# Attention followed by a max-of-three feed-forward: the last 64 queries summed in 64x64 tiles, and output tiles stored by one transfer

## Chip, cores and metric

The kernel runs on one core of one Trainium2 chip. The metric is the device time in microseconds (us). The kernel before took 341.37 us (median of 8 runs, 341.04 to 341.73).

## What is computed

`q`, `k` and `v` have 8 batches, 12 heads, 448 positions and head size 64, in float32. The attention is a softmax whose denominator has one more term; its result is laid out as 3584 tokens of 768 features and goes through a feed-forward part with three weight matrices and a maximum.

```python
scores = scale * np.matmul(q, k.transpose(0, 1, 3, 2))      # scale = 1/8
m = np.max(scores, axis=-1, keepdims=True)
e = np.exp(scores - m)
attn = e / (np.sum(e, axis=-1, keepdims=True) + np.exp(-m) + 1e-09)
x = np.matmul(attn, v)                                       # to (3584, 768)
h = np.maximum(np.maximum(x @ w1, x @ w2), x @ w3)
out = h @ w_out
```

## The kernel before

All matmuls are in float16 with float32 sums. The kernel leaves the maximum out: it computes exp(scores) and divides by the sum plus 1, which is the same quotient but for the 1e-09. Values carry a 65th column of 1/256, so that one matmul gives the weighted sum and the denominator, both scaled alike (L161, L162).

**Groups.** The 12 heads of a batch go in 3 groups of 4 heads, so there are 24 groups `i`. The 448 positions are taken as 7 rows of 64. The 4 heads are two pairs `pr`, and the 4 windows `w` of a head's queries hold 128, 128, 128 and 64 queries: the last window is half empty. Keys are taken in blocks of two rows of 64 (X1, X2, X3 in L274) and one tail row `TL`, for which both heads of a pair share one block.

**One group.** Loads come from GpSimd's queue (`load_qk`, `load_v`), three to four groups ahead, and cast to float16. From group 7 on two DMA transposes on SyncE's queue (SP) turn queries and keys (`transpose_dma`, L233, issued two groups ahead), and GpSimd shifts parts of the queries between partition halves (`shift_q`, four copies, L245). Scores (L300) are 64x64 tiles of TensorE, their exponential is ScalarE's (L320) and is written to one of two buffers `e`.

**Attention times values.** `av` (L528) works on one pair of heads and one accumulator tile `avp`, which is two PSUM banks from a pool of three tiles shared with the scores. `av_tail` (L330) adds the tail row for the four windows as 16 tiles of 64x64. `av_main` (L349) adds the three full blocks as 2 heads x 4 windows x 3 blocks = 24 matmuls of 128x128 by 65 columns. VectorE then computes the denominators (L367), their reciprocals (L370) and the product for all four windows and both heads (L373), into `xn`.

**Feed-forward.** `xn` of a group goes to `xT`, from group 6 on by one DMA transpose on SP (`x_transpose_dma`, L421). The work of the feed-forward is cut in pieces: `up_piece` is six matmuls into one of two PSUM tiles of the pool `ps_b` and a copy or a running maximum by VectorE (L449, L451); `out_piece` is six matmuls for half of a 128-row output tile (L464), scaled by VectorE into one of six buffers `o_sb` (L471). After the second half the tile is stored.

**Order.** The order is written by hand. Each group `i` from 3 on has three visits `vi` with 2, 2 and 3 score units (loop at L620). The first two visits also run `av` of the group before. After that `fill` (L511) issues pieces from a list until a credit in matmul columns is used up; `share` (L606) spreads what is left evenly over the visits up to the next batch. The engines work through their own instructions in this order. At the end (L670) come the two last `av`, the last transpose of `xn`, the rest of the pieces and those of the last batch.

**Stores.** A 128-row output tile holds two rows of 64 tokens, whose places in the output are 7 tokens apart, and the two halves start at different tokens. Each half is stored by its own transfer of 64 partitions, both from SP (L481); the last tile goes in three cuts, partly from ScalarE's queue.

Of the kernel before, what the change touches and what calls it, by code (L numbers as in the profile page):

```python
# [10 lines left out]
FP32 = mybir.dt.float32  # L11
FP16 = mybir.dt.float16
AF = mybir.ActivationFunctionType
ALU = mybir.AluOpType
ts = bass.ts

MMDT = FP16
# [4 lines left out]
def kernel(  # L22
# [33 lines left out]
    PE_QK = 7  # L56
    NF = 3
    PE_X = 2
    NEB = 2
    NV = 3  # L60

    cpool = ctx.enter_context(tc.tile_pool(name="const", bufs=1))
    att_pool = ctx.enter_context(tc.tile_pool(name="att", bufs=3))
    small = ctx.enter_context(tc.tile_pool(name="small", bufs=3))
    xn_pool = ctx.enter_context(tc.tile_pool(name="xn", bufs=3))
    xt_pool = ctx.enter_context(tc.tile_pool(name="xt", bufs=3))
    ht_pool = ctx.enter_context(tc.tile_pool(name="ht", bufs=2))
    out_pool = ctx.enter_context(tc.tile_pool(name="outp", bufs=6))
# [94 lines left out]
    for j in range(NEB):  # L163
        nc.vector.memset(e_buf[j][:, NB * S : NB * S + HP], 0.0)
        blk = e_buf[j][:, 0 : NB * S].rearrange("p (n s) -> p n s", s=2 * S)
        nc.vector.memset(blk[:, :, NO : NO + HP], 0.0)

    def warm(n, cols=512):
        ps = ps_b.tile([128, 512], FP32, tag="b", name="warm")
# [152 lines left out]
    def e_col(n, w):  # L322

        return n * S + ((192, 320, 0, 128) if n % 2 == 0 else (0, 128, 256, 384))[w]
# [5 lines left out]
    def av_tail(i, ej, pr, ws=(0, 1, 2, 3)):  # L330

        eF, vt = e_buf[ej], vt_buf[i % NV]
        ps = ps_s.tile([128, 2, 512], FP32, tag="s", name="avp")
        avs[i, pr] = ps
        n = where[pr, None, TL]
        for j, w in enumerate(ws):
            for hh in range(2):
                for half in range(2):
                    o = e_col(n, w) + half * HP
                    nc.tensor.matmul(  # L340
                        out=ps[half * HP : half * HP + HP, hh, j * D1 : (j + 1) * D1],
                        lhsT=eF[hh * HP : hh * HP + HP, o : o + HP],
                        rhs=vt[hh * HP : hh * HP + HP, pr, 0:D1],
                        start=(j == 0),
                        stop=False,
                        skip_group_check=True,
                    )

    def av_main(i, ej, pr, ws=(0, 1, 2, 3)):  # L349
        eF, vx = e_buf[ej], v_buf[i % NV]  # L350
        ps = avs.pop((i, pr))
        nw = len(ws)
        for hh in range(2):
            for j, w in enumerate(ws):
                for c, x in enumerate((X1, X3, X2)):
                    o = e_col(where[pr, hh, x], w)
                    nc.tensor.matmul(  # L357
                        out=ps[:, hh, j * D1 : (j + 1) * D1],
                        lhsT=eF[:, o : o + 128],
                        rhs=vx[:, 2 * pr + hh, (x[0]), 0:D1],  # L360
                        start=False,
                        stop=(c == 2),
                        skip_group_check=True,
                    )
        acc = ps[:, :, 0 : nw * D1].rearrange("p h (j d) -> p h j d", d=D1)
        rb = small.tile([P, 2, 4], FP32, tag="rb", name="rb")
        nc.vector.tensor_scalar(  # L367
            out=rb[:, :, 0:nw], in0=acc[:, :, :, D], scalar1=1.0 / LAMBDA, scalar2=None, op0=ALU.add
        )
        nc.vector.reciprocal(out=rb[:, :, 0:nw], in_=rb[:, :, 0:nw])  # L370
        if i not in xn:
            xn[i] = xn_pool.tile([P, NP, 4, 2, D], MMDT, tag="xn", name="xn")
        nc.vector.tensor_tensor(  # L373
            out=xn[i][:, pr, ws[0] : ws[0] + nw].rearrange("p j h d -> p h j d"),
            in0=acc[:, :, :, 0:D],
            in1=rb[:, :, 0:nw].unsqueeze(3).to_broadcast([P, 2, nw, D]),
            op=ALU.mult,
        )

    def prep_v(i, eng):  # L380
        t = raw[i]["v"]
        vx, vt = v_buf[i % NV], vt_buf[i % NV]
        eng.tensor_copy(out=vx[:, :, :, 0:D], in_=t[:, :, 1:4, :])  # L383
        t2 = t.rearrange("p (r h) t d -> p r h t d", r=NP)
        eng.tensor_copy(out=vt[0:HP, :, 0:D], in_=t2[0:HP, :, 0, 4, :])
        eng.tensor_copy(out=vt[HP:P, :, 0:D], in_=t2[HP:P, :, 1, 0, :])
# [34 lines left out]
    def x_transpose_dma(i):  # L421
        b, g = groups[i]
        nc.sync.dma_start_transpose(
            out=xt_tile(b)[:, 2 * g : 2 * g + 2, :].rearrange("p a (j s) -> p (a j) s", s=128),
            in_=xn[i].rearrange("p a j h d -> p (a j h d)"),
        )
# [26 lines left out]
    NW = DM // 2  # L453
    order = (0, 2, 4, 6, 1, 3, 5)

    def out_piece(bp, t, c, w, queues):

        if c == 0:
            outs[0] = out_pool.tile([128, DM], FP32, tag="o_sb", name="o_sb")
            outs[1] = 0  # L460
        o_sb = outs[0]
        op_ps = ps_b.tile([128, 512], FP32, tag="b", name="op_ps")
        for fc in range(NFC):
            nc.tensor.matmul(  # L464
                out=op_ps[:, 0:w],
                lhsT=hT[bp][:, fc, ts(t, 128)],
                rhs=wout_sb[:, fc, c : c + w],
                start=(fc == 0),
                stop=(fc == NFC - 1),
            )  # L470
        nc.vector.tensor_scalar(  # L471
            out=o_sb[:, c : c + w], in0=op_ps[:, 0:w], scalar1=1.0 / LAMBDA, scalar2=None,
            op0=ALU.mult,
        )
        if queues is None:
            return
        for half in range(2):
            n = 2 * t + half
            b = 2 * bp + n // T
            rows = out[b * S : (b + 1) * S].rearrange("(p t) m -> t p m", t=T)[order[n % T]]  # L480
            queues[half].dma_start(  # L481
                out=rows[:, outs[1] : c + w], in_=o_sb[half * HP : half * HP + HP, outs[1] : c + w]
            )
        outs[1] = c + w


# [9 lines left out]
    def add_out(b):  # L496
        sy, sc = nc.sync, nc.scalar
        for t in range(0, 3) if b % 2 == 0 else range(3, 7):
            cuts = [(0, NW, None), (NW, NW, (sy, sy))]
            if b == B - 1 and t == 6:  # L500
                cuts = [(0, NW, (sy, sy)), (NW, 256, (sc, sc)), (NW + 256, 128, (sy, sc))]
            for c, w, queues in cuts:
                pieces.append((out_piece, (b // 2, t, c, w, queues), NFC * (w + 6)))

    def add_batch(b):
        add_up(b, 0, S, [(i, fc) for fc in range(NFC) for i in range(3)])
# [4 lines left out]
    def fill(cols):  # L511
# [5 lines left out]
        if not pieces:  # L517
            credit[0] = min(credit[0], 0.0)

    def left():  # L520
        return sum(w for _, _, w in pieces)

# [3 lines left out]
    STEP = 2 * NDC * (NO + 6)  # L526

    def av(i, ej, pr, part):  # L528
        av_tail(i, ej, pr, PW[part])
        av_main(i, ej, pr, PW[part])  # L530

# [88 lines left out]
    for i in range(3, NI):  # L620
        ej, pj = (i + 1) % NEB, i % NEB
        first = i == 3
        if PE_QK <= i + 2 < NI:
            transpose_dma(i + 2)
        if first:
            load_v(i + 2)
        for vi, units in enumerate(visits):
            n = 3 * i + vi
            scores(i, ej, units)
            if i == 4 and vi == 0:  # L630
                prep_v(i, DV)
            if vi < 2:
                av(i - 1, pj, vi, "E" if first else "EO")
            if vi == 1 and i > 3 * PE_X:
                x_transpose_dma(i - 1)
            if n in adds:
                add_batch(adds[n])
            per = STEP if first and vi < 2 else share(n)
            if vi == 0 and first:
                x_transpose_pe(1, "E")  # L640
            if vi == 2 and first:
                x_transpose_pe(i - 1, "E")
                fill(per / 2)
                prep_v(i, DV)
                for w, cols in ((0, (0, NE)), (1, (0, NE)), (2, (NE, NO)), (2, (0, NE))):
                    add_up(0, *cols, [(w, f) for f in (0, 2, 4)])
                add_out(0)
                per = share(n)
            if vi == 2 and 3 < i <= 3 * PE_X:
                x_transpose_all(i - 1)  # L650
            if first:
                fill(per)
                per = 0
            if i + 1 < PE_QK and vi < 2:
                transpose_once(i + 1, "qk"[vi], (AC, DV)[vi])
            fill(per)
        if i + 1 < PE_QK:
            shift_q(i + 1, nc.gpsimd)
        if first:
            load_qk(i + 3)  # L660
        if i < 5:
            load_more(i + 3, i + 4)
        if 5 <= i + 1 < NI:
            prep_v(i + 1, nc.gpsimd)
        if PE_QK <= i + 2 < NI:
            shift_q(i + 2, nc.gpsimd)
        if i >= 5:
            load_more(i + 3, i + 4)

    av(NI - 1, NI % NEB, 0, "EO")  # L670
    av(NI - 1, NI % NEB, 1, "EO")
    x_transpose_dma(NI - 1)
    fill(float("inf"))
    add_batch(B - 1)
# [31 lines left out]
```

The softmax here doesn't subtract the row's maximum and nothing guards it: scores larger than these inputs give would overflow.

## Time and profile before

| | us |
|---|---|
| median of 8 runs (range) | 341.37 (341.04 to 341.73) |
| profiled execution, its own time | 341.04 |
| its span, first to last instruction | 339.2 |
| TensorE busy, matmuls | 329.2 |
| VectorE busy | 188.5 |
| ScalarE busy | 151.1 |
| GpSimd busy | 146.4 |

The profile is one execution with times from the hardware. "L357" is a line of the kernel; `avp<-vx,e` names what is written and read. PE is TensorE's matmuls, PEld its weight loads, DVE VectorE, ACT ScalarE, POOL GpSimd, SPq the queue of SyncE. A group's line gives the count, the busy time, the mean of one in ns, and the idle time before it with what ended it. Matmuls overlap in a pipeline, so the pace of a row of them is read from the starts, and not from the mean of one. The mean granted clock of TensorE was 0.999 of full speed. DMA lines give a queue's packets, megabytes, and the time that its packets took as a share of the 16 DMA engines; issue lines give the count, the size of one and the median time from issue to landing.

### The profile page before, as it was taken

The numbers are of one execution on the slowest core, as the hardware profiler recorded it, in microseconds if no ns is written. First come the engines' busy times: TensorE is split into PE (matmuls) and PEld (weight loads), VectorE is DVE, ScalarE is ACT, GpSimd is POOL, SyncE is SP. The second block draws the span as 40 slices with busy tenths as digits, with TensorE's granted clock in tenths as the row PEclk, the third lists the DMA queues.
The fourth block names the chain that finished last, engine by engine and source line by source line (L and its number), as shares of the span: only waits on it lengthen the run. The fifth ranks groups of instructions, "written<-read, shape, count | busy, mean of one in ns | idle before, by whom it ended". The sixth has DMA issues, their size and how long they took to land.

```text
span 339.2 us, 9812 instructions
## 1 busy us (share of the span) xinstructions
PE 329.2 (97%) x4172; PEld 198.9 (59%) x4172; DVE 188.5 (56%) x410; ACT 151.1 (45%) x181; POOL 146.4 (43%) x260
## 2 busy tenths in 40 slices
PE   7899999999999999999999999999999999999994
PEld 3678788765555655555555645555555655555552
DVE  4556665565546555555545555546456556465552
ACT  4868856653554545453543445463543454200000
POOL 8595669882735177065265271936162000000000
PEclk9999999999999999999999999999999999999999
DMA  8999999999997997989988999999960440133006
GB/s 148 194 186 206 201 206 179 151 165 206 126 128 107 216 213 103 127 135 208 138 102 108 209 199 106 156 138 197 150 119 20 116 116 3 31 79 95 0 19 167
DMA packets 84812, 46.42 MB, mean 137 GB/s; under 512 B 53280, under 2 KB 81312, under 8 KB 84768
## 3 DMA queue, kind: packets, MB, share of 16 engines
q0 software_dynamic: 29120, 21.80, 48.2%
q1 hardware_dynamic: 55264, 23.60, 38.1%
q8 instruction: 32, 0.52, 0.6%
q10 hardware_dynamic: 384, 0.39, 0.4%
q14 instruction: 12, 0.10, 0.1%
HBM read 44.04 MB, written 11.01 MB: 162 GB/s over the span
## 4 chain that ended last, share of the span: by engine, by line
PE 91%; ACT 2%; DVE 2%; DMA 2%; issue 1%; POOL 1%; POOLq 0%; ACTq 0%
PE p_i L440 48%; PE op_ps L464 16%; PE avp L357 11%; PE stp L300 11%; PE avp L340 2%; ACT e L320 2%; DMA ld_q<-in_q_dram 2%; DVE xn L373 1%; PE trT L225 1%; DVE QT L186 1%; PE xtp L413 0%; ACT QT L184 0%; DVE rb L370 0%; POOL ld_k L102 0%; PE xtp L400 0%
## 5 line engine op out<-in xcount | busy, mean ns | idle before, releaser
L320 ACT ACTIVATE e<-stp 128x896 f16<-128x896 f32 (+4 forms) x171 | 144.2, 904 | 137.0 <-PE stp L300 136.8
L440 PE MATMUL p_i<-xT,w 128*128 128x448 f16 (+2 forms) x972 | 173.4, 332 | 0.2
L440 PEld LDWEIGHTS <-w 128*128 128x128 f16 x972 | 90.0, 98 | 68.2 <-issue 5.4
L245 POOL COPY QT<-QT 64x384 f16<-64x384 f16 (+1 forms) x84 | 46.7, 556 | 93.5 <-DMA QT<-ld_q 71.6
L451 DVE TENSOR_TENSOR hT<-hT,p_i 128x448 f16<-128x448 f16 (+2 forms) x96 | 59.6, 621 | 43.1 <-PE p_i L440 42.9
L464 PE MATMUL op_ps<-w,hT 128*128 128x384 f16 (+2 forms) x342 | 58.1, 323 | 0.0
L300 PE MATMUL stp<-QT,KT 64*64 64x448 f16 (+2 forms) x756 | 48.1, 338 | 2.6 <-ACT e L320 0.9
L464 PEld LDWEIGHTS <-hT 128*128 128x128 f16 x342 | 32.1, 98 | 23.0 <-issue 2.0
L357 PE MATMUL avp<-vx,e 128*128 128x65 f16 x1152 | 45.4, 193 | 0.0
L471 DVE TENSOR_SCALAR o_sb<-op_ps 128x384 f32<-128x384 f32 (+2 forms) x57 | 31.3, 550 | 23.7 <-PE op_ps L464 23.1
L449 DVE CAST hT<-p_i 128x448 f16<-128x448 f32 (+2 forms) x48 | 30.0, 625 | 24.4 <-PE p_i L440 24.4
L357 PEld LDWEIGHTS <-e 128*128 128x128 f16 x1152 | 38.8, 97 | 2.3
L373 DVE TENSOR_TENSOR xn<-avp,rb 128x512 f16<-128x512 f32 (+1 forms) x54 | 34.1, 632 | 1.9
L300 PEld LDWEIGHTS <-KT 64*64 64x64 f16 x756 | 15.9, 105 | 27.1 <-issue 24.3
L367 DVE TENSOR_SCALAR rb<-avp 128x8 f32<-128x8 f32 (+1 forms) x54 | 8.9, 165 | 40.2 <-PE avp L357 40.1
L383 POOL COPY vx<-ld_v 128x768 f16<-128x768 f16 x21 | 17.2, 818 | 7.6 <-issue 4.4
L340 PEld LDWEIGHTS <-e 64*64 64x64 f16 x768 | 14.8, 107 | 7.9 <-issue 1.4
L102 POOL DMA_DIRECT2D ld_q<-in_q_dram x24 | 17.5, 730 | 2.5 <-DMA w<-in_moe_w_out_dram 1.7
L102 POOL DMA_DIRECT2D ld_k<-in_k_dram x24 | 17.4, 727 | 2.1 <-PE p_i L440 1.3
L115 POOL DMA_DIRECT2D ld_v<-in_v_dram x24 | 15.2, 634 | 3.2 <-DMA w<-in_moe_w_dram 1.9
L340 PE MATMUL avp<-vt,e 64*64 64x65 f16 x768 | 15.4, 192 | 0.6 <-ACT e L320 0.4
L112 POOL DMA_DIRECT2D ld_v<-in_v_dram x24 | 15.2, 635 | 1.6 <-DMA w<-in_moe_w_dram 1.6
(43 smaller groups left out, 86.0 us busy)
## 6 DMA issues: line engine op xcount, KB each, us to landing
out_dram<-o_sb SPq DMA_DIRECT2D x54, 192.0 KB, 3.5
ld_v<-in_v_dram POOLq DMA_DIRECT2D x48, 128.0 KB, 4.3
ld_k<-in_k_dram POOLq DMA_DIRECT2D x23, 224.0 KB, 6.6
ld_q<-in_q_dram POOLq DMA_DIRECT2D x23, 224.0 KB, 7.0
w<-in_moe_w_dram POOLq DMA_DIRECT2D x9, 384.0 KB, 9.4
w<-in_moe_w_out_dram POOLq DMA_DIRECT2D x3, 384.0 KB, 8.7
xT<-xn SPq DMA_TRANSPOSE x18, 3.9
QT<-ld_q SPq DMA_TRANSPOSE x17, 5.0
```

Source lines behind the costliest of these rows:

```text
L102: nc.gpsimd.dma_start(out=tiles[nm][:, 1 : NP * T + 1].rearrange("x (r t) d -> x r (t d)", r=NP)[:, p0:p1], in_=src[:, p0:p1],)
L245: eng.tensor_copy(out=t[d0 : d0 + HP, o * 128 : (o + n) * 128], in_=t[s0 : s0 + HP, a * 128 : (a + n) * 128],)
L300: nc.tensor.matmul(out=stp[half * HP : half * HP + HP, par, j * qn : (j + 1) * qn], lhsT=k_block(i, pr, h2, x[half]), rhs=q_cols(i, pr, h2 ...
L320: nc.scalar.activation(out=dst, in_=src, func=AF.Exp, scale=scale)
L340: nc.tensor.matmul(out=ps[half * HP : half * HP + HP, hh, j * D1 : (j + 1) * D1], lhsT=eF[hh * HP : hh * HP + HP, o : o + HP], rhs=vt[hh * ...
L357: nc.tensor.matmul(out=ps[:, hh, j * D1 : (j + 1) * D1], lhsT=eF[:, o : o + 128], rhs=vx[:, 2 * pr + hh, (x[0]), 0:D1], start=False, stop= ...
L373: nc.vector.tensor_tensor(out=xn[i][:, pr, ws[0] : ws[0] + nw].rearrange("p j h d -> p h j d"), in0=acc[:, :, :, 0:D], in1=rb[:, :, 0:nw]. ...
L440: nc.tensor.matmul(out=p_i[:, j * qn : (j + 1) * qn], lhsT=w_sb[i][:, dc, ts(fc, 128)], rhs=xT[b][:, dc, q0 : q0 + qn], start=(dc == 0), s ...
L449: nc.vector.tensor_copy(out=dst, in_=src)
L451: nc.vector.tensor_tensor(out=dst, in0=dst, in1=src, op=ALU.max)
L464: nc.tensor.matmul(out=op_ps[:, 0:w], lhsT=hT[bp][:, fc, ts(t, 128)], rhs=wout_sb[:, fc, c : c + w], start=(fc == 0), stop=(fc == NFC - 1),)
L471: nc.vector.tensor_scalar(out=o_sb[:, c : c + w], in0=op_ps[:, 0:w], scalar1=1.0 / LAMBDA, scalar2=None, op0=ALU.mult,)
```

## The change

There are two parts.

*Sums of the last window.* From group 6 on (`LAST`), `av_tail` and `av_main` cover windows 0 to 2 alone. A new function `av_last` computes window 3 as 64x64 tiles: the contraction's two halves go to two row halves of TensorE and to two banks, and the two heads to two partition halves. So each bank holds half of the sum. ScalarE copies the second bank's half out of PSUM (`end`); one piece of the feed-forward is issued (`one`); then `finish` lets VectorE add the first bank's half, compute the denominator and reciprocal, and ScalarE scale the two heads into `xn`. The transpose of `xn` is issued after `finish`. The unused partitions of `xn` are set to zero once, so `xn` becomes three fixed buffers.

*Stores.* An output tile is stored by one transfer with a target of two runs of 64 rows, where the second half's token follows the first's (`r1 > r0`); otherwise by two transfers as before. Of seven tiles per two batches one (t = 5) stays with two.

```diff
@@ setup
+    LAST = 6
...
-    xn_pool = ctx.enter_context(tc.tile_pool(name="xn", bufs=3))
...
+    xn_buf = [cpool.tile([P, NP, 4, 2, D], MMDT, name=f"xn{j}") for j in range(NV)]
+    for j in range(NV):
+        nc.vector.memset(xn_buf[j][HP:P, :, 3], 0.0)
@@ new
+    def av_last(i, ej, pr):
+        eF, vx, vt = e_buf[ej], v_buf[i % NV], vt_buf[i % NV]
+        ps = avs[i, pr]
+
+        def tile_mm(r, hh, o, rhs, stop):
+            nc.tensor.matmul(
+                out=ps[hh * HP : hh * HP + HP, r, 3 * D1 : 4 * D1],
+                lhsT=eF[r * HP : r * HP + HP, o : o + HP],
+                rhs=rhs,
+                start=False,
+                stop=stop,
+                skip_group_check=True,
+            )
+
+        n = where[pr, None, TL]
+        for hh in range(2):
+            tile_mm(hh, hh, e_col(n, 3), vt[hh * HP : hh * HP + HP, pr, 0:D1], False)
+        for c, x in enumerate((X1, X3, X2)):
+            for r in range(2):
+                for hh in range(2):
+                    o = e_col(where[pr, hh, x], 3)
+                    rhs = vx[r * HP : r * HP + HP, 2 * pr + hh, x[0], 0:D1]
+                    tile_mm(r, hh, o, rhs, c == 2)
@@ av_main, after the product for the windows given
+        if not last:
+            return None
+        end = small.tile([P, D1], FP32, tag="end", name="end")
+        rl = small.tile([P, 1], FP32, tag="rl", name="rl")
+        nc.scalar.activation(out=end, in_=ps[:, 1, 3 * D1 : 4 * D1], func=AF.Copy)
+
+        def finish():
+            nc.vector.tensor_tensor(out=end, in0=ps[:, 0, 3 * D1 : 4 * D1], in1=end, op=ALU.add)
+            nc.vector.tensor_scalar(
+                out=rl, in0=end[:, D:], scalar1=1.0 / LAMBDA, scalar2=None, op0=ALU.add
+            )
+            nc.vector.reciprocal(out=rl, in_=rl)
+            for hh in range(2):
+                h = slice(hh * HP, hh * HP + HP)
+                nc.scalar.activation(
+                    out=xn[i][0:HP, pr, 3, hh], in_=end[h, 0:D], func=AF.Copy, scale=rl[h]
+                )
+
+        return finish
@@ out_piece
-        for half in range(2):
-            n = 2 * t + half
-            b = 2 * bp + n // T
-            rows = out[b * S : (b + 1) * S].rearrange("(p t) m -> t p m", t=T)[order[n % T]]
-            queues[half].dma_start(
-                out=rows[:, outs[1] : c + w], in_=o_sb[half * HP : half * HP + HP, outs[1] : c + w]
-            )
+        r0, r1 = ((2 * bp + n // T) * S + order[n % T] for n in (2 * t, 2 * t + 1))
+        cols = slice(outs[1], c + w)
+        for p0, r, k in ((0, r0, 2),) if r1 > r0 else ((0, r0, 1), (HP, r1, 1)):
+            at = out[r : r + 1, cols]
+            rows = bass.AP(
+                at.tensor, at.offset, [[abs(r1 - r0) * DM, k], [T * DM, HP], [1, c + w - outs[1]]]
+            )
+            queue.dma_start(out=rows, in_=o_sb[p0 : p0 + k * HP, cols])
@@ add_out: the last tile's cuts
-                cuts = [(0, NW, (sy, sy)), (NW, 256, (sc, sc)), (NW + 256, 128, (sy, sc))]
+                cuts = [(0, NW, sy), (NW, 256, sc), (NW + 256, 128, sy)]
@@ planner
+    def one():
+        if pieces:
+            fill(max(0.0, 1.0 - credit[0]))
...
     def av(i, ej, pr, part):
+        if i >= LAST:
+            av_tail(i, ej, pr, (0, 1, 2))
+            av_last(i, ej, pr)
+            return av_main(i, ej, pr, (0, 1, 2), True)
@@ loop over visits
+            finish = None
             if vi < 2:
-                av(i - 1, pj, vi, "E" if first else "EO")
-            if vi == 1 and i > 3 * PE_X:
-                x_transpose_dma(i - 1)
+                finish = av(i - 1, pj, vi, "E" if first else "EO")
             if n in adds:
                 add_batch(adds[n])
             per = STEP if first and vi < 2 else share(n)
+            if finish:
+                one()
+                finish()
+            if vi == 1 and i > 3 * PE_X:
+                x_transpose_dma(i - 1)
@@ end
-    av(NI - 1, NI % NEB, 0, "EO")
-    av(NI - 1, NI % NEB, 1, "EO")
+    for pr in range(NP):
+        finish = av(NI - 1, NI % NEB, pr, "EO")
+        one()
+        finish()
     x_transpose_dma(NI - 1)
```

More of the change, by code (lines that the diff above doesn't have):

```diff
@@ L347, in av_tail, with av_main @@
                     )
-    def av_main(i, ej, pr, ws=(0, 1, 2, 3)):
+    def av_last(i, ej, pr):
[19 more added lines that the diff above has]
+                    tile_mm(r, hh, o, rhs, c == 2)
+    def av_main(i, ej, pr, ws=(0, 1, 2, 3), last=False):
         eF, vx = e_buf[ej], v_buf[i % NV]
@@ L365, in av_main @@
         acc = ps[:, :, 0 : nw * D1].rearrange("p h (j d) -> p h j d", d=D1)
-        rb = small.tile([P, 2, 4], FP32, tag="rb", name="rb")
+        rb = small.tile([P, 2, nw], FP32, tag=f"rb{nw}", name="rb")
         nc.vector.tensor_scalar(
-            out=rb[:, :, 0:nw], in0=acc[:, :, :, D], scalar1=1.0 / LAMBDA, scalar2=None, op0=ALU.add
+            out=rb, in0=acc[:, :, :, D], scalar1=1.0 / LAMBDA, scalar2=None, op0=ALU.add
         )
-        nc.vector.reciprocal(out=rb[:, :, 0:nw], in_=rb[:, :, 0:nw])
+        nc.vector.reciprocal(out=rb, in_=rb)
         if i not in xn:
-            xn[i] = xn_pool.tile([P, NP, 4, 2, D], MMDT, tag="xn", name="xn")
+            xn[i] = xn_buf[i % NV]
         nc.vector.tensor_tensor(
@@ L375, in av_main @@
             in0=acc[:, :, :, 0:D],
-            in1=rb[:, :, 0:nw].unsqueeze(3).to_broadcast([P, 2, nw, D]),
+            in1=rb.unsqueeze(3).to_broadcast([P, 2, nw, D]),
             op=ALU.mult,
         )
+        if not last:
[15 more added lines that the diff above has]
+        return finish
     def prep_v(i, eng):
@@ L454, with out_piece @@
     order = (0, 2, 4, 6, 1, 3, 5)
-    def out_piece(bp, t, c, w, queues):
+    def out_piece(bp, t, c, w, queue):
         if c == 0:
@@ L474, in out_piece @@
         )
-        if queues is None:
+        if queue is None:
             return
-        for half in range(2):
-            n = 2 * t + half
-            b = 2 * bp + n // T
-            rows = out[b * S : (b + 1) * S].rearrange("(p t) m -> t p m", t=T)[order[n % T]]
-            queues[half].dma_start(
-                out=rows[:, outs[1] : c + w], in_=o_sb[half * HP : half * HP + HP, outs[1] : c + w]
+        r0, r1 = ((2 * bp + n // T) * S + order[n % T] for n in (2 * t, 2 * t + 1))
[4 more added lines that the diff above has]
+                at.tensor, at.offset, [[abs(r1 - r0) * DM, k], [T * DM, HP], [1, c + w - outs[1]]]
             )
+            queue.dma_start(out=rows, in_=o_sb[p0 : p0 + k * HP, cols])
         outs[1] = c + w
@@ L498, in add_out @@
         for t in range(0, 3) if b % 2 == 0 else range(3, 7):
-            cuts = [(0, NW, None), (NW, NW, (sy, sy))]
+            cuts = [(0, NW, None), (NW, NW, sy)]
             if b == B - 1 and t == 6:
-                cuts = [(0, NW, (sy, sy)), (NW, 256, (sc, sc)), (NW + 256, 128, (sy, sc))]
-            for c, w, queues in cuts:
-                pieces.append((out_piece, (b // 2, t, c, w, queues), NFC * (w + 6)))
+                cuts = [(0, NW, sy), (NW, 256, sc), (NW + 256, 128, sy)]
+            for c, w, queue in cuts:
+                pieces.append((out_piece, (b // 2, t, c, w, queue), NFC * (w + 6)))
     def add_batch(b):
```

## The prediction

> **What bounds the kernel now.** I read the busy table first, then TensorE's own waits, then the busy time and DMA share by stage, then single stretches of TensorE, then the DMA queues of the middle stage.
>
> ```profile
> PE 329.2 (97%) x4172; PEld 198.9 (59%) x4172; DVE 188.5 (56%) x410; ACT 151.1 (45%) x181; POOL 146.4 (43%) x260
> ```
> ```profile
> PE stp L300 <- ACT e L320: 0.9, 3, 0.4
> ...
> PE avp L340 <- ACT e L320: 0.4, 1, 0.4
> ```
> ```profile
> core 0: us, PE busy (x) PEld busy (x) DVE busy (x) ACT busy (x) POOL busy (x), PEclk, DMA share, GB/s
> ...
> 67.00:254.00 187.00, 187.00 (x2330) 105.91 (x2326) 104.20 (x211) 88.96 (x106) 93.56 (x169) 1.00 1.06 153
> 254.00:300.00 46.00, 46.00 (x582) 26.56 (x567) 26.17 (x55) 17.90 (x21) 2.88 (x6) 1.00 0.22 53
> 300.00:339.00 39.00, 34.28 (x198) 18.75 (x195) 19.70 (x34) 0.00 (x0) 0.00 (x0) 0.99 0.30 78
> ```
> TensorE has no gap from 67 to 300 us: its work is the time. But in the middle stage the DMA share is 1.06 (packet times include waiting, so they can exceed 1): the second thing near its limit is DMA, until the last loads are in at about 254 us.
>
> One attention-times-values step (`av`) in the steady part:
> ```profile
> 207.19 0.20 PE L340 MATMUL avp<-vt,e 64*64 64x65 f16 x4
> ...
> 207.19 0.23 PE L340 MATMUL avp<-vt,e 64*64 64x65 f16 x8
> ...
> 207.19 0.26 PE L340 MATMUL avp<-vt,e 64*64 64x65 f16 x12
> ...
> 207.19 0.29 PE L340 MATMUL avp<-vt,e 64*64 64x65 f16 x16
> 207.42 0.93 PE L357 MATMUL avp<-vx,e 128*128 128x65 f16 x24
> 208.18 2.43 PE L440 MATMUL p_i<-xT,w 128*128 128x448 f16 x12
> ```
> Four 64x64 tiles together cost 0.03 us (each window that takes in four more ends 0.03 later). The 24 full matmuls take 208.18 - 207.42 = 0.76, so 0.032 each. The step takes 0.99.
>
> The DMA queues from 67 to 254 us (packets, MB, share of 16 engines; then issues, KB, us to landing), and a stretch of 0.8 us at 119.6 in which nearly only stores run:
> ```profile
> q1 hardware_dynamic: 45346, 17.24, 54.7%
> q0 software_dynamic: 16715, 11.00, 50.4%
> ...
> out_dram<-o_sb SPq DMA_DIRECT2D x34, 192.0 KB, 4.6
> ...
> QT<-ld_q SPq DMA_TRANSPOSE x15, 5.1
> ...
> xT<-xn SPq DMA_TRANSPOSE x14, 4.4
> ```
> ```profile
> q1 hardware_dynamic: 117, 0.31, 97.5%
> ```
> The second shows an engine's pace: 16 x 0.975 x 0.8 = 12.5 engine-us for 0.31 MB. A tile of 128 rows (393 KB) is 15.8 engine-us. The packet records say 121 ns for a 3072-byte packet (median), so 15.5 in all; I use that.
>
> [...] In the kernel before every store has 64 rows outermost on both sides; no run here shows a smaller one. [...] the last 64x64 tile and the first full matmul are 0.125 us apart. [...] The 896-wide exponential took 917 ns here[...].
>
> **The change, part by part.**
>
> *Tiles for the last 64 queries (36 steps: groups 6 to 23, two pairs).* Removed per step: 4 of 16 tail tiles (one slot of 0.03) and 6 of 24 full matmuls (0.19). Added: 14 tiles; [...] 4 slots, 0.12. Both orders change modes equally often. Net -0.10 us, x 36 = **-3.6 us**, all of it on TensorE's path. Bounds: if the repeated sums into one address ran at 0.04 a slot, -2; if the odd pair shared a slot, -4.5.
>
> *VectorE.* The product shrinks from 512 to 384 elements (0.69 to about 0.56 from the 256- and 512-wide rows), and three small operations come in: a sum over 65 (about 0.23 by the same line) and two on one element (nearest row: 0.16 and 0.18 at 4). Net +0.4 x 36 = 14 us on an engine 56% busy. The sum comes after one more piece: evacuated by about 1.8 us after the step, the sum done by 2.1. What waits for it is the accumulator's bank, next used by the following visit 2.3 us after the step at the earliest (two output pieces of 0.98, then scores). Covered; without cover 0.3 us a visit.
>
> *ScalarE.* [...] The copy waits for TensorE and, by the instruction order, also for VectorE's product; behind it stand the next visit's exponentials, which come 2 us later and have over 2 us until TensorE needs them. I take 0.
>
> *Planner and transposes.* Pieces are only reordered. The transpose of `xn` is issued about 1.7 us later (after the scaled copies) on SP, ahead of the query and key transposes and stores; these have 12 us or more, except at the end. There it would be issued 3.0 us after the last step and landed by 5.7 (2.7 in that window); six output pieces cover 5.9 and four matmuls more 0.75. I take 0. The three memsets (about 0.16 each, between the rows of 85 and 245 ns) lie in VectorE's wait of 1.9 us for the first load.
>
> *Stores.* 23 tiles, and the three cuts of the last tile, leave as one transfer each; every seventh tile still as two. The new transfer's target is written as [2, 64, columns], its source as 128 rows. [...] k = 2: such a tile takes 15.5 / 2 = **7.7 us on two engines** instead of 1 us on sixteen. These two also carry their share of all loads and transposes.
>
> Work of such an engine between 67 and 254 us, at waiting-free packet times (packet records: 60 ns for 512 bytes, 88 for 896, 18 for 256): loads 72 us, transposes 46, stores (2176 packets of 3072 bytes before, 17 tiles; 15 of them now on two engines) 15 x 7.7 + 2 = 118. Sum 237 in 187 us: **50 us too much**. [...] The query transposes are issued two groups ahead (two batches span 77.2 us in the chain, so 25.7); less landing (5.1) and the four shifts on GpSimd (0.56 each), 18 us of backlog can be put off past 254 us, where DMA is idle. That leaves 32; chained waits (output buffers, six of them, hold up VectorE, then the two accumulators of the pieces) add some: I take **+40**. Bounds: 0 if nearly all of it can be put off; +107 if packets keep the full shares shown (105.1% of 187 less 21 us of stores, plus 118: 294).
>
> *End.* After the last step TensorE needs 5.9 + 20.4 + 8.1 = 34.4 us (chain). The first full store of the last batch is ready at 26.4 + 2.7 = 29.0, its packets start 1.1 later (as before), two such stores end at 45.6, the split tile at 46.6, and the last tile's 64 packets each of 65, 46 and 26 ns (1536, 1024 and 512 bytes) at 55.4: 21.0 after TensorE's end. Before, the last packet ended at 337.46, 3.2 after TensorE's 334.28. So **+17.8 us**. Were k 16, fewer issues (the last pair ends 1 us earlier) would give about -0.7.
>
> Sum: the profiled span 339.2 - 3.6 + 40 + 17.8 = 393.4. Outside the span lie 341.04 - 339.2 = 1.8, and the median of the runs is 0.3 above the profiled one: **395.5 us**.
>
> **Rivals.**
> - *Not slower: the stores spread over 16 engines after all.* One mechanism, the number of engines for a target of [2, 64, columns]; it decides from k = 8 or so, where a tile takes 2 us like the output pieces that make it. For it: 128 rows on the other side, and no run here with a small outer dimension. [...] Then 339.2 - 3.6 - 0.7 + 2.1 = 337.0.
> - *Two engines, but the middle absorbs it.* For it: six output buffers, loads issued three groups ahead. Against it: 237 us of work in 187. Only the end pays: 355.5.
> - *Sixteen engines and a late bank:* 0.3 us in 18 visits, 342. Against it is the margin worked out above.
>
> **How the numbers follow.** Forecast 0.70, middle absorbed 0.08, sixteen engines 0.19 (plus 0.01 with no change left), late bank 0.02. A change within 0.2% can't be told from none. Faster 0.19, same 0.01, slower 0.80. The forecast's own range is 356 to 445 (0 to about 90 us in the middle). To leave out no more than 2 in 10 the range must reach the sixteen-engine case: 336.5 to 420, where the upper end (65 us in the middle) leaves out about 0.17.
>
> **What would show it.** Right: stores of 128 rows land 8 us or more after issue, those of 64 rows don't follow from their size; packets run on for 20 us after TensorE; VectorE and TensorE get waits for `out_dram`, `xT` or `QT` between 67 and 254; the step takes 0.89. Wrong: landing stays near 4 us and TensorE stays without gaps; then the gain of 3.6 stands alone.

## The result and the profile after

The changed kernel took 415.98 us (median of 11 runs, 413.18 to 417.1); beside it the kernel before took 341.31. The ratio is 1.2174, 95% interval 1.2158 to 1.2191: 74.7 us slower, and 20.5 more than the 395.5 forecast. The profiled execution took 417.1, its span 415.3. A run that is over 1.5% longer than the fastest of its kernel is left out of comparisons; this concerns one run of experiment A, whose median it moves by 0.05 us, and one of M.

The page of the changed kernel, with its busy times, its TensorE clock in 40 slices of the span, and the line of the new stores:

```profile
PE 338.5 (82%) x4316; PEld 200.8 (48%) x4316; DVE 199.2 (48%) x521; ACT 183.1 (44%) x289; POOL 146.4 (35%) x260
...
PEclk9999999999995798999889998899967999999955
...
out_dram<-o_sb SPq DMA_DIRECT2D x23, 384.0 KB
```
TensorE is now idle 18% of the span. It also has more busy time than before (338.5 against 329.2), though it has less to do; the reason is in the row under it: its clock is below full speed in many slices from 125 us on (a slice is 10.4 us). The line of the new stores carries no time to landing, so one of the prediction's signs, a landing of 8 us or more, can't be read; for the old stores the page says 3.5 us.

The waits of the changed kernel (us in total, times, longest):

```profile
POOL QT L249 <- DMA QT<-ld_q: 162.2, 11, 25.8
...
PE stp L304 <- DMA KT<-ld_k: 24.9, 4, 13.1
...
PE p_i L490 <- DMA xT<-xn: 17.2, 2, 16.0
```
Before, TensorE waited for nothing from 67 us on. Now it waits up to 13 and 16 us, and 42.1 of its 49.7 us of gaps after 60 us are waits for transposes. None is put down to a store or an output buffer. Two gaps of 2.8 us (157.3 and 262.5) are put down to nothing. Each ends 1.3 to 1.5 us after a 16 KB packet of the instruction queue that took 2.6 and 3.0 us; before, none took over 1.7. That TensorE waited for its own instructions there is likely, not shown.

Its stages, with the columns shown for the kernel before (the first pair of numbers in a row is PE busy; the last three are clock, DMA share, GB/s):

```profile
67.00:254.00 187.00, 155.78 (x1995) 86.74 (x1992) 90.62 (x238) 92.80 (x153) 67.87 (x122) 0.92 1.17 110
254.00:300.00 46.00, 38.89 (x441) 20.34 (x439) 22.24 (x58) 21.26 (x36) 14.18 (x26) 0.94 1.07 110
300.00:339.00 39.00, 27.68 (x334) 15.68 (x335) 14.67 (x40) 15.52 (x26) 14.51 (x27) 0.82 1.08 108
339.00:415.00 76.00, 53.82 (x476) 29.85 (x474) 32.47 (x70) 9.66 (x19) 0.00 (x0) 0.87 0.36 57
```
The DMA share stays above 1 until 339 us, where it fell to 0.22 at 254 before, and yet fewer bytes move: 110 GB/s for 153. So packets spend their time waiting; experiment J looks at what they wait for.

DMA from 340 us to the end, first the busy tenths in 40 slices of 1.9 us, then GB/s:

```profile
DMA  1911115930007111111111111011167211111110
GB/s 52 116 49 52 52 52 130 66 66 0 0 3 150 26 47 61 52 52 52 52 52 52 52 52 52 31 26 51 52 111 168 60 49 51 52 51 51 51 46 15
```
The digit 1 is a share of one eighth, two engines of sixteen (from 370 to 385 us the packet records add up to 0.129), and what they move then is 52 GB/s. A tile of 393 KB at that pace takes 7.6 us; the prediction had 7.7. This is the direct sign that a target of [2, 64, columns] runs on two engines in this kernel. No run before it showed one with a small outermost dimension, so the k = 2 of the prediction, the number of engines, was the author's assumption.

From the matmul records, adding up every stretch over 0.03 us without one:

| us | before | after | difference |
|---|---|---|---|
| TensorE without a matmul | 5.1 | 54.3 | +49.2 |
| TensorE with a matmul | 329.2 | 338.5 | +9.3 |
| TensorE's last matmul ends | 334.3 | 392.8 | +58.5 |
| from there to the last packet | 3.2 | 21.3 | +18.1 |

With the tile sums alone (experiment A) the second row is 326.25. So +9.3 is -3.0 of work saved and +12.3 by which the same work took longer; the clock records account for 10.8 of these (21.6 us of work at half clock). The whole is -3.0 + 49.2 + 12.3 + 18.1 = 76.6, less 0.5 for a shorter tail after the last packet: the span grew by 76.1.

One `av` step, in A, where the clock is full:

```profile
207.19 0.26 PE L344 MATMUL avp<-vt,e 64*64 64x65 f16 x12
...
207.51 0.73 PE L388 MATMUL avp<-vx,e 128*128 128x65 f16 x18
208.08 2.24 PE L490 MATMUL p_i<-xT,w 128*128 128x448 f16 x11
```
The step took 0.99 before; now it is 208.08 - 207.19 = 0.89. The 14 tiles take the four slots of the forecast: in the changed kernel they start at 104.83 in groups of 4, 4, 4 and 2, about 0.03 us apart, and the first full matmul follows the last tile's start by 0.124 us (0.126 before).

### The profile page after: what moved, and what is told of

It is laid out like the page before. It is cut to its first block, busy times and chain, and to the rows that moved or that the text cites. A ratio compares the mean times of both kernels' runs of the same rounds, so it can differ in the third digit from the quotient of the medians.

```text
span 415.3 us, 10220 instructions
## 1 busy us (share of the span) xinstructions
PE 338.5 (82%) x4316; PEld 200.8 (48%) x4316; DVE 199.2 (48%) x521; ACT 183.1 (44%) x289; POOL 146.4 (35%) x260
## 4 chain that ended last, share of the span: by engine, by line
PE 40%; DMA 33%; POOL 10%; SPq 8%; issue 2%; ACT 1%; DVE 1%; POOLq 0%
PE p_i L490 20%; DMA QT<-ld_q 13%; PE op_ps L514 10%; DMA KT<-ld_k 8%; SPq L241 6%; PE stp L304 4%; DMA ld_q<-in_q_dram 4%; PE avp L388 4%; DMA w<-in_moe_w_dram 4%; POOL QT L249 2%; DMA w<-in_moe_w_out_dram 2%; DMA ld_v<-in_v_dram 2%; POOL ld_k L102 2%; POOL ld_q L102 1%; POOL vx L433 1%
## 5 line engine op out<-in xcount | busy, mean ns | idle before, releaser
L490 PE MATMUL p_i<-xT,w 128*128 128x448 f16 (+2 forms) x972 | 179.2, 339 | 20.3 <-DMA xT<-xn 17.2
L304 PE MATMUL stp<-QT,KT 64*64 64x448 f16 (+2 forms) x756 | 50.6, 346 | 29.1 <-DMA KT<-ld_k 24.9
L514 PE MATMUL op_ps<-w,hT 128*128 128x384 f16 (+2 forms) x342 | 60.1, 328 | 2.8 <-issue 2.8
L424 ACT ACTIVATE xn<-end,rl 64x64 f16<-64x64 f32 x72 | 24.9, 346 | 54.4 <-DVE rl L421 53.9
L398 DVE TENSOR_SCALAR rb<-avp 128x6 f32<-128x6 f32 (+2 forms) x54 | 8.8, 164 | 66.3 <-PE avp L388 66.2
L388 PE MATMUL avp<-vx,e 128*128 128x65 f16 x936 | 39.9, 197 | 0.0
L388 PEld LDWEIGHTS <-e 128*128 128x128 f16 x936 | 33.2, 99 | 2.4
L404 DVE TENSOR_TENSOR xn<-avp,rb 128x384 f16<-128x384 f32 (+2 forms) x54 | 29.3, 543 | 1.8
L433 POOL COPY vx<-ld_v 128x768 f16<-128x768 f16 x21 | 17.2, 818 | 4.8 <-DMA ld_v<-in_v_dram 3.9
L414 ACT ACTIVATE end<-avp 128x65 f32<-128x65 f32 x36 | 8.2, 226 | 19.5 <-PE p_i L490 10.6
L115 POOL DMA_DIRECT2D ld_v<-in_v_dram x24 | 15.2, 634 | 2.2 <-DMA w<-in_moe_w_dram 1.3
```

The source lines that it names most:

```text
L304: nc.tensor.matmul(out=stp[half * HP : half * HP + HP, par, j * qn : (j + 1) * qn], lhsT=k_block(i, pr, h2, x[half]), rhs=q_cols(i, pr, h2 ...
L388: nc.tensor.matmul(out=ps[:, hh, j * D1 : (j + 1) * D1], lhsT=eF[:, o : o + 128], rhs=vx[:, 2 * pr + hh, (x[0]), 0:D1], start=False, stop= ...
L404: nc.vector.tensor_tensor(out=xn[i][:, pr, ws[0] : ws[0] + nw].rearrange("p j h d -> p h j d"), in0=acc[:, :, :, 0:D], in1=rb.unsqueeze(3) ...
L490: nc.tensor.matmul(out=p_i[:, j * qn : (j + 1) * qn], lhsT=w_sb[i][:, dc, ts(fc, 128)], rhs=xT[b][:, dc, q0 : q0 + qn], start=(dc == 0), s ...
L514: nc.tensor.matmul(out=op_ps[:, 0:w], lhsT=hT[bp][:, fc, ts(t, 128)], rhs=wout_sb[:, fc, c : c + w], start=(fc == 0), stop=(fc == NFC - 1),)
```

## The experiments

All times are compared with the kernel before on the same chip (341.2 to 341.3); a ratio is to that kernel and comes with its 95% interval. "Gaps" are the stretches of TensorE without a matmul after 60 us.

### A. The tile sums alone

The changed kernel with the old stores:

```diff
-        for p0, r, k in ((0, r0, 2),) if r1 > r0 else ((0, r0, 1), (HP, r1, 1)):
+        for half in range(2):
...
+            queues[half].dma_start(
```


> The changed kernel with the stores of the kernel before (two transfers of 64 rows, old queues). Theory 1 (the new stores run on two DMA engines, and all of the loss is theirs): the tile sums alone gain 36 steps x 0.10 us, so 341.3 - 3.6 = 337.7 us, no new waits of TensorE. Rival (the later bank and the longer ScalarE and VectorE chain carry part of the loss): 342 us or more.

Measured: 338.97 (20 runs, ratio 0.9936, interval 0.9925 to 0.9947), 2.2 us faster. TensorE's busy time fell by 3.0. The rest was given back in two places: TensorE waits 0.53 us for `xT` at 118.25, and the last packet comes 3.5 instead of 3.2 us after TensorE. SP's issues around that wait (start, time held):

```profile
108.68 1.11 SPq L531 DMA_DIRECT2D out_dram<-o_sb  x2
109.94 2.35 SPq L473 DMA_TRANSPOSE xT<-xn  x1
```
From the issue of the transpose at 109.94 to the matmul that needs it at 118.25 there are only 8.3 us. That number matters below.

### B. The stores alone

The kernel before with the new `out_piece` and the new cuts:

```diff
-            cuts = [(0, NW, None), (NW, NW, (sy, sy))]
+            cuts = [(0, NW, None), (NW, NW, sy)]
```


> The kernel before with the new stores alone (one transfer with a target of 2 x 64 rows). Theory 1: the loss of 74.7 us plus the 3.6 that the tile sums gave, so about 416 + 3.6 = 420 us. Rival (the loss needs both parts, since the later transposes of xn meet the stores): well below 400 us.

Measured: 417.87 (ratio 1.2263, 1.2206 to 1.2321), with 40.6 us of gaps and packets that run on 21.4 us after TensorE. Of these gaps 23.1 us are waits for transposes, and 17.0 are put down to nothing, as the two in the changed kernel. Theory 1 holds: the loss, 76.7 us here and 77.0 between A and the changed kernel, is in the stores; the tile sums have no part in it.

### C. One transfer of 128 rows, with the 64 rows outermost

The same number of transfers, the same bytes, the same rows of the output; only the order of the target's dimensions is turned. So that the source's partitions come in that order, VectorE writes the two token rows of an output tile interleaved into `hT`, in two instructions per piece.

```diff
-                at.tensor, at.offset, [[abs(r1 - r0) * DM, k], [T * DM, HP], [1, c + w - outs[1]]]
+                at.tensor, at.offset, [[T * DM, HP], [abs(r1 - r0) * DM, k], [1, c + w - outs[1]]]
```


> The changed kernel with the same number of transfers and bytes, but the 64 rows outermost in the target (64 x 2 x columns): the two halves of a tile are laid alternately on the partitions, by VectorE writing h with a step of 2, in two instructions a piece. Theory 1 (the outermost size of 2 sets the number of engines): stores run on 16 engines again, landing near 4 us, time 337 to 339 us. Rival (one transfer of 128 rows is slow or blocks its queue whatever its pattern): 400 us or more.

Measured: 336.93 (ratio 0.9899, 0.9866 to 0.9932). There is no gap after 60 us, and the page of C shows the stores land:

```profile
out_dram<-o_sb SPq DMA_DIRECT2D x23, 384.0 KB, 4.5
```
A transfer of 128 rows isn't slow as such (4.5 us to landing here); one whose target has 2 outermost is (7.6 us a tile at the pace of the changed kernel). C is also the fastest kernel of this study, 4.3 us under the kernel before.

### D. C's stores in the kernel before

The edit of C without the tile sums.

> The kernel before with only the other stores: one transfer per tile with 64 rows outermost and the two runs second, the rows of h interleaved by VectorE; no tile sums. If those stores are worth what they differ by with the tile sums in (336.93 against 338.97): 339 to 340. If that difference was only the wait for xT and the spread of the runs: 341.3 within 0.3.

Measured: 339.45 (ratio 0.9951, 0.9935 to 0.9968), 1.7 us faster. The last packet ends 2.1 us after TensorE instead of 3.2; there are half as many issues at the end. So C's gain is 2.2 from the sums and about 2 from the stores. The prediction gave stores on sixteen engines -0.7.

### E. All stores from ScalarE's queue

```diff
-            cuts = [(0, NW, None), (NW, NW, sy)]
+            cuts = [(0, NW, None), (NW, NW, sc)]
...
-                cuts = [(0, NW, sy), (NW, 256, sc), (NW + 256, 128, sy)]
+                cuts = [(0, NW, sc), (NW, 256, sc), (NW + 256, 128, sc)]
```


> The changed kernel with all stores issued from ScalarE's queue, so that transposes on SyncE's queue do not stand behind them. If the order within a queue's ring makes the middle loss: the waits for KT, QT and xT go, about 50 us come back, 360 to 368 us (the end still costs 18). If the two engines are simply short of time (237 us of work in 187): the loss stays, over 395 us. [...] ScalarE is held at its issues and the exponentials come late: also slow, but with waits for ScalarE instead.

Measured: 438.86 (2 runs, ratio 1.2868, 1.2783 to 1.2954): 22.9 us worse than the changed kernel, so the first expectation is out. Its waits:

```profile
ACT e L324 <- issue: 22.2, 6, 8.3
PE stp L304 <- ACT e L324: 20.1, 16, 5.1
...
PE p_i L490 <- DMA xT<-xn: 14.9, 5, 9.6
```
The transposes have a queue without stores now. TensorE's waits for them fell from 42.1 to 14.9 us, but did not go, and others came in their place. ScalarE, which has exponentials to do, is held at the issue of its stores (one issue takes up to 6.6 us while TensorE is at work, and 8.3 pass between two exponentials at 224.9), and TensorE pays 20.1 for that. So the order within the queue probably has a large part in the waits for transposes (with TensorE held elsewhere they also had more time), and the third expectation comes nearest: a slow kernel with waits for ScalarE. What the two engines' shortage of time would cost alone, with stores on a queue that holds up nothing, no run shows. SP's transposes are still held at their issue up to 10.7 us here, against 4.3 at most before, though no store stands in their queue.

### F and G. The end and the rest, apart

F keeps two rows outermost only in the last tiles of the last pair of batches; G is the complement.

```diff
-        for p0, r, k in ((0, r0, 2),) if r1 > r0 else ((0, r0, 1), (HP, r1, 1)):
+        for p0, r, k in ((0, r0, 2),) if r1 > r0 and (bp == B // 2 - 1 and t >= 3) else ((0, r0, 1), (HP, r1, 1)):
```
```diff
-        for p0, r, k in ((0, r0, 2),) if r1 > r0 else ((0, r0, 1), (HP, r1, 1)):
+        for p0, r, k in ((0, r0, 2),) if r1 > r0 and not (bp == B // 2 - 1 and t >= 3) else ((0, r0, 1), (HP, r1, 1)):
```


> The changed kernel, but only the last pair of batches' tiles from t = 3 on (and the last tile's three cuts) keep the target of two rows outermost; every other tile is stored as two transfers of 64 rows. If the end is paid by itself, because two engines hold a queue of 7.7 us per tile when TensorE stops: 338.97 (tile sums alone) plus about 17, so 354 to 358, packets that run on some 20 us after TensorE, and no TensorE gap before 300 us. If the late end is only a consequence of the delayed middle stage: 339 to 345.

> The complement: two rows outermost everywhere except in those last tiles. If the middle and the end add up: 416 less 17, so 396 to 401, TensorE gaps of some 49 us with its granted clock near 0.92, and packets that end within 5 us of TensorE. If the two interact (the backlog of the middle reaches the end), more than 405.

Measured: F 356.21 (ratio 1.0435, 1.0398 to 1.0472), G 399.27 (1.1696, 1.1611 to 1.178). Against A, F loses 17.2; against the changed kernel, G gains 16.7. End and middle add up. F's DMA from 333 us to its end shows the end alone, in GB/s over slices of 0.55 us:

```profile
GB/s 56 56 45 95 163 151 247 172 88 67 51 65 45 49 56 49 56 45 60 45 49 56 45 71 56 45 56 45 50 50 50 50 50 50 45 43 43 11 0 0
```
TensorE is done at 332.1, and two engines at 50 GB/s need until 353.4. G keeps the gaps of the middle, 48.8 us, and its stores end 3.7 us after TensorE.

### H. Two slow tiles of seven

```diff
-        for p0, r, k in ((0, r0, 2),) if r1 > r0 else ((0, r0, 1), (HP, r1, 1)):
+        for p0, r, k in ((0, r0, 2),) if r1 > r0 and (bp < B // 2 - 1 and t in (0, 3)) else ((0, r0, 1), (HP, r1, 1)):
```


> Two rows outermost in only two of seven tiles (t = 0 and 3) of the first three pairs of batches, six transfers in all; the rest are pairs of 64 rows. The busiest engine's work from 67 to 254 us is then 72 (loads) + 46 (transposes) + 6 x 7.7 + 11 x 1 = 175 us, under the 187 there are. If the middle costs only what exceeds the stage's length: 339 to 342. If each such transfer costs TensorE its own wait (61 us for 15 of them in the middle, so 4 each): about 363.

Measured: 350.92 (ratio 1.028, 1.0213 to 1.0346), between the two expectations: both miss. There is one gap, 10.7 us at 119.3, for `xT`; the other slow stores cost nothing. A sum over the stage can't give this: the expectation left the busiest engine 12 us to spare, and in fact 18, since the sixth slow store is issued at 276 us, after that stage.

### J and K. The six slow stores taken apart

J keeps one of the six, the tile t = 3 of the first pair of batches; K keeps the other five.

```diff
-        for p0, r, k in ((0, r0, 2),) if r1 > r0 else ((0, r0, 1), (HP, r1, 1)):
+        for p0, r, k in ((0, r0, 2),) if r1 > r0 and (bp == 0 and t == 3) else ((0, r0, 1), (HP, r1, 1)):
```
```diff
-        for p0, r, k in ((0, r0, 2),) if r1 > r0 else ((0, r0, 1), (HP, r1, 1)):
+        for p0, r, k in ((0, r0, 2),) if r1 > r0 and (bp < B // 2 - 1 and (t == 0 or bp > 0 and t == 3)) else ((0, r0, 1), (HP, r1, 1)):
```


> One single transfer with two rows outermost: the tile t = 3 of the first pair of batches. In the run with six of them this store was issued at 109.74 us, a transpose of xn 1.3 us behind it in the same queue, and TensorE waited 10.7 us for that transpose; it is the only wait. If the cost is a matter of what stands directly behind a slow store: the whole 11 us come from this one, so 348 to 351, with one gap of about 10 us near 119. If it is a backlog that several slow stores build up: 339 to 342, no gap above 2 us.

> The other five of those six transfers, without the one of the run beside it. If what stands directly behind a store decides: 339 to 341.5, no gap above 1 us. If a backlog of several decides: some 347 to 350.

Measured: J 350.83 (ratio 1.028, 1.026 to 1.0301), K 338.29 (0.9913, 0.9893 to 0.9933). A single slow store out of 28 tiles costs 11.9 us against A; five others cost nothing. SP's issues in J, and the transposes of `xn` between 90 and 140 us:

```profile
109.52 0.62 SPq L534 DMA_DIRECT2D out_dram<-o_sb  x1
110.78 1.64 SPq L473 DMA_TRANSPOSE xT<-xn  x1
```
```profile
DMA to landing us min/median/max: 4.2/5.5/16.9
```
J's DMA from 109 to 130 us, in slices of 0.53 us:

```profile
DMA  9981205759999911111011119999999999999996
GB/s 224 24 136 23 23 15 51 45 108 149 124 125 96 57 50 41 41 41 41 28 31 41 41 31 116 85 85 97 92 119 128 165 140 294 291 266 297 236 192 225
```
The transpose is issued 1.3 us behind the slow store, lands 16.9 us after its issue, at 127.7, and TensorE needs it at 119.1. In the "DMA" row a packet's time counts in the slice in which the packet begins. So the row of ones, 116.4 to 121.6, says only that hardly any packets begin; the two engines with the store go on. The other engines are not free. J's packets that begin between 114.0 and 116.4 (packets, MB, share of 16 engines):

```profile
q1 hardware_dynamic: 309, 0.19, 346.3%
```
A share of 346% means that packets outlast the window. At 119.0, 18 of the transposes' 256-byte packets are under way, whose median time is 0.018 us before. They began by 116 and all end within 0.05 us of 121.74, which is 0.3 us after the slow store's last packet. Meanwhile the loads of the next groups stand nearly still as well. So this transpose, behind a slow store, ties up the other engines for as long as the store still needs. The packet records show the same in every run with slow stores in SP's queue ahead of transposes. Stretches after 60 us with at least eight such packets, each of which takes over 3 us, add up to 10.1 us in J and to 95.8 in the changed kernel, where loads move 2.6 GB/s in them (59 in the middle stage before). The kernel before, A, C, D and L have none, and E, with the stores in another queue, has a single one of 3.2. Why these packets hang together no run shows.

K has 16.6 us of such stretches and loses nothing. Behind four of its five slow stores come other stores and then a transpose of queries, which is needed two groups later; behind the fifth, at 262.7 us, the next transpose of `xn` is issued only 10 us later. In these runs it takes both, the standstill and a transpose that is needed at once.

J also shows what a gap costs beyond itself (TensorE's busy time, then clock in the third column from the end):

```profile
119.00:127.70 8.70, 0.09 (x2) 0.00 (x1) 0.35 (x1) 0.65 (x2) 0.00 (x0) 0.67 1.04 118
127.70:129.70 2.00, 2.00 (x6) 0.86 (x6) 0.99 (x4) 0.00 (x0) 0.00 (x0) 0.50 1.84 241
129.70:131.70 2.00, 2.00 (x7) 0.76 (x5) 0.71 (x2) 0.69 (x2) 0.00 (x0) 0.50 0.73 131
131.70:133.70 2.00, 2.00 (x19) 0.74 (x18) 0.62 (x1) 0.65 (x1) 0.40 (x1) 0.89 1.13 263
133.70:135.70 2.00, 2.00 (x12) 1.08 (x11) 0.62 (x1) 1.89 (x3) 1.84 (x5) 1.00 1.03 203
```
After the gap of 8.6 us TensorE runs at half its clock for more than 4 us, and so loses (2 + 2) x 0.5 + 2 x 0.11 = 2.2 us.

### L. Gaps without slow stores

C with one output buffer in place of six:

```diff
-    out_pool = ctx.enter_context(tc.tile_pool(name="outp", bufs=6))
+    out_pool = ctx.enter_context(tc.tile_pool(name="outp", bufs=1))
```


> A test of the clock, apart from slow stores: the version with 64 rows outermost in one transfer (336.93), but with one output buffer in place of six, so that VectorE waits for each store to land and TensorE behind it. If gaps in TensorE's work by themselves bring the granted clock down as in the changed kernel (0.92 with 49 us of gaps), the clock falls in proportion to the gaps here too, to some 0.95 for 30 us. If the lower clock comes from the two-engine stores or the long single gaps of 8 to 16 us: 0.99 or more whatever the gaps. By 28 tiles with 2 to 3 us of uncovered wait the time would be 370 to 420 with the former.

Measured: 393.99 (ratio 1.1541, 1.1443 to 1.164). VectorE waits 70.7 us for stores, TensorE's gaps are 38.6 us in sum (the longest 6.3), and its clock is 0.946: busy time for the same work rises from 326.1 to 343.7. The stores land in 2.9 us here. So gaps are enough for a lower clock here, without slow stores. One of only 2.8 us is followed by half the clock:

```profile
116.20:119.00 2.80, 0.01 (x1) 0.01 (x2) 0.62 (x2) 2.18 (x3) 2.70 (x5) 1.00 0.93 134
119.00:121.00 2.00, 2.00 (x10) 1.08 (x10) 0.40 (x1) 0.00 (x0) 1.95 (x4) 0.79 1.11 129
121.00:123.00 2.00, 2.00 (x37) 0.95 (x35) 0.00 (x0) 0.54 (x1) 0.88 (x3) 0.50 0.97 141
```

### M. All slow stores but those ahead of a transpose of xn

G with six more tiles stored as pairs of 64 rows:

```diff
-... if r1 > r0 and not (bp == B // 2 - 1 and t >= 3) else ...
+... if r1 > r0 and not (bp == 3 and t >= 3) and (bp, t) not in ((0, 3), (0, 6), (1, 2), (1, 6), (2, 2), (2, 6)) else ...
```


> The run that kept two rows outermost everywhere except in the last tiles (399.27), with six more tiles stored as pairs of 64 rows: those that stand directly ahead of a transpose of xn in SP's queue (t = 3 and 6 of the first pair of batches, 2 and 6 of the second and third). Fifteen slow stores remain. If the middle's loss is made by these six places: 339 to 345. If it is an excess of engine time: the busiest engine has 72 + 46 + 10 x 7.7 + 7 x 1 = 202 us in 187, 15 too much, so 352 to 360. If every slow store costs its share: 338.97 + 15/21 of 60, about 382.

Measured: 357.33, 18.4 over A and 42 under G; the other run took 365.75. A single run lies in the 352 to 360 of the excess of engine time, and both are far from 342 and from 382. What G pays for those six places can't be split further by this: taking them away removes six badly placed stores and also some 5 x 6.7 = 34 us of work from the two engines between 67 and 254 us.

## Why the prediction was right and where it was not

*Two engines.* Right. 52 GB/s on an eighth of the engines (after), 7.6 us a tile; C, which moves the same bytes in as many transfers with the 64 rows outermost, has none of it. The rival with sixteen engines is out.

*The end, +17.8.* Right: 18.1 by the last packet, 17.2 and 16.7 in F and G. The rival in which only the end pays, 355.5, is what F measures with 356.21; it is not the changed kernel, whose middle pays as well.

*The middle, +40.* This is the step that failed; between A and the changed kernel it was +61, namely 49.1 us more of gaps and 12.3 of slower work. One term was missing, and another was reckoned with too few engines and too much time to spare.

The missing term is TensorE's clock. The prediction took the same work at full speed. It took 12.3 us longer in the changed kernel, 13.2 in G and 17.0 in B, of which the clock records account for 10.8, 12.1 and 14.9. L shows gaps doing this without any slow store (38.6 us of them, clock 0.946), J shows the 2.2 us after one of them.

The other is "50 us too much" less "18 us of backlog can be put off past 254 us". The excess of engine time, worked out as in the prediction, stands beside what was measured (all in us but the first column of numbers; "standing still" are the stretches described at J):

| run | slow tiles from 67 to 254 us | work of the busiest engine | excess over 187 | standing still | gaps | slower work |
|---|---|---|---|---|---|---|
| A | 0 | 135 | 0 | 0 | 0.6 | 0 |
| K | 4 | 162 | 0 | 16.6 | 0.1 | 0 |
| J | 1 | 142 | 0 | 10.1 | 9.3 | 3.1 |
| H | 5 | 169 | 0 | 27.4 | 10.7 | 1.8 |
| B | 15 | 237 | 50 | 99.4 | 40.6 | 17.0 |
| G | 15 | 237 | 50 | 93.4 | 48.8 | 13.2 |
| changed kernel | 15 | 237 | 50 | 95.8 | 49.7 | 12.3 |

The work counts 72 + 46 for loads and transposes, 7.7 for a slow tile and 1 for another of the 17. The sum charges two engines alone, but behind a slow store the transposes hold the others too, and J and H lose time without any excess. The argument for putting off looked at the transposes of queries, which have 25.7 us, and left out those of `xn`, issued by the same SP and needed after 8.3 (A, J). It also took SP's issue for free. An issue of the kernel before, then those of the changed kernel (start and time held):

```profile
183.91 1.23 SPq L423 DMA_TRANSPOSE xT<-xn  x1
```

```profile
116.50 0.52 SPq L534 DMA_DIRECT2D out_dram<-o_sb  x1
117.11 8.51 SPq L473 DMA_TRANSPOSE xT<-xn  x1
125.72 4.99 SPq L534 DMA_DIRECT2D out_dram<-o_sb  x3
130.88 7.82 SPq L241 DMA_TRANSPOSE QT<-ld_q  x1
```
A transpose's issue that took 1.2 us in most cases before, and never over 4.3, is held for 8 here, and everything after it in SP's order starts later. So slack of one transfer is used up by the others.

That the gaps come so near the excess of 50 in the changed kernel and G is partly luck. B, with the same stores, has 40.6, which is the forecast's 40, and still loses as much in all. J's loss is shown to come from its place; how much of the changed kernel's 49.7 is place and how much excess is not settled, for M changes both. Luck has a part in the total too. It lies 4 us inside the range, whose upper end of 65 us in the middle came from the chances given; the clock, 12 of the 61 us, was in no term.

*"Chained waits (output buffers, six of them, hold up VectorE)".* Not found: no wait of VectorE for `out_dram` stands in the changed kernel's list. As the new stores' landings are not in the profile, such a wait could lack its name; but each of the 57 copies into `o_sb` starts within 0.25 us of the last matmul that it reads or of VectorE's operation before it.

*Tile sums, -3.6.* Right in kind: 0.09 a step for the 0.10, and -3.0 of busy time. A's time gained 2.2.

*ScalarE, VectorE and the late bank, 0.* Right: the copy took 226 ns and a scaled copy 346 (changed kernel), so 0.92 us a step, and A shows no wait for the accumulator's bank.

*The later transpose of xn, 0.* Nearly: 0.5 us in A, at the one place with 8.3 us of cover. The prediction examined that transpose's cover only at the end.

## What to carry to other kernels

Before merging transfers, look at the outermost dimension of the target: here the merged transfer had half the issues and an eighth of the engines, and the same merge with the 64 rows outermost made the kernel 1% faster instead of 22% slower. When engine time is short, don't ask how long the average transfer may be put off, but which of those sharing the engines and the issuing queue is needed soonest, here 8.3 us after its issue. A store on two engines ahead of a transpose in one queue took the time of the other engines too: 10.1 us of standing still for the one slow store of J. And price a stall of TensorE above its length: 49 us of gaps came with 12 us of slower work here, and 39 us in many short ones with 18.

## What the runs showed that was not expected

- The slow store of one tile of 28 can cost 11.9 us by its place (J), and five like it nothing (K).
- With slow stores under way the issuing engine was held at its issues: a transpose of queries up to 16.9 us at SP in the changed kernel (4.3 before), a store up to 6.6 us at ScalarE in E while TensorE was at work.
- Behind a store on two engines, a transpose's packets hung on the other engines until the store was done (J, to within 0.3 us), and loads nearly stopped (2.6 GB/s in such stretches of the changed kernel, 95.8 us in all).
- A gap of TensorE of 2.8 us already brought half the clock for some microseconds (L).
